# Block sums of w2 by accumulating transfers in GpSimd's queue, and the signs of seven products

## The chip, the cores and the metric

The kernel runs on one core of one Trainium2 chip. The metric is device time in microseconds (us) of one execution. The profiler records one further execution; its span is the time from the first to the last recorded instruction. PE is TensorE, DVE VectorE, ACT ScalarE, POOL GpSimd; SP issues the transfers of the kernel before.

## The reference

A layer norm feeds a linear attention block and a GELU feed-forward block; the second gates the first. S = 2048 rows, D = 576, 32 heads of 18, F = 4608, all in float32.

```python
x = A_x
xn = _layernorm(x, axis=-1)
s = _A_ref(xn, A_wqkv, A_wo)                     # phi(q) (phi(k)^T v) / (phi(q) sum phi(k)), then @ wo
h = gelu(xn @ w1 + b1)                           # 2048 x 4608
g = silu(h @ w2 + b2)                            # 2048 x 576
return x + s * g
```

## The kernel before

Float32 products are made on PE from split operands: `hi` is the value rounded by ACT to the type that PE multiplies, `lo` is the remainder, subtracted by DVE; a product is hi·hi + hi·lo + lo·hi. The large products are cut into 2 x 2 blocks and made with seven block products in place of eight (Strassen's scheme in Winograd's form), so sums of blocks of each operand are wanted as operands too. The second feed-forward product, `h @ w2`, takes four 128-row tiles of F at a time: a chunk `c` of nine. Its w2 operand has four blocks B(r, n) of 128 x 2 x 288 values in SBUF, r the row half and n the column half, and three sums of them.

The program has three stages.

1. **Keys and values** (to about 160 us): eight pairs of 128-row tiles. For a pair the rows are normalized (`x_stats`, with a power on POOL, L245; `x_norm` on ACT, L260), transposed on PE (`transpose_x`, L270), split and summed (`x_sum`, `s_hi`, `s_lo`), and projected. `s_lo` (L317 and L321) subtracts the remainders of x's sums on DVE.
2. **Queries and attention** (to about 290 us): rounds r = 0 to 9 of 14 places each. A round projects one pair's queries, divides (`den_sum` on DVE, `den_div` on POOL, L817), transposes the result of the pair before (L834, into one PSUM tile that `th` on ACT, L841, and `tl`, `th` on DVE, L845 and L846, must empty before the next), and multiplies it by the folded weights.
3. **Feed-forward**: 18 steps of 28 places, nine chunks for each half of the rows. A step makes two `Up` groups of seven products (`h`, L1118, with DVE's combinations L1138 to L1155 and the GELU on ACT, L1126), then, from place 14 on, the seven products with w2 (L1255), drained into `macc` by DVE (L1262).

Sums of w2's blocks are made at two places. `w2_load`, `w2_sum`, `w2_hi`, `w2_lo` (L473 to L503) run in stages 1 and 2: `SUMS` lists 19 (chunk, product) pairs, j = 0 to 18, and each is loaded, subtracted on POOL (L492), split on ACT (L496) and DVE (L501), and stored to DRAM. Class `W2` (from L1165) makes the others in the first half of stage 3, for the next chunk, as `sum7` (one subtraction, L1171) and `sum4` (two in a row, L1176 and L1177); `hi` and `lo` (L893, L896) split each operand, and the second half of the rows reads what was stored.

The order of work is written out by hand: `add(place, function, ...)` puts a function at a place, `at_step(place)` runs what stands there after a piece of PE's work, and every compute engine runs its own instructions strictly in that order, waiting at each until its inputs are there. In stages 1 and 2 this holds for the transfers of SP as well. The places of w2's sums:

```python
W2_FIRST = {2: (0,), 3: (1, 2), 4: (3,), 5: (4, 5), 6: (6,)}   # stage 1: pair -> sums j
    add(base + (1, 3)[n], w2_sum, j)
    add(base + (4, 9)[n], w2_hi, j)
    add(base + (6, 12)[n], w2_lo, j)
    add(base + ((0, 3) if r > 2 else (4, 5))[j], w2_sum, n + j)   # stage 2, rounds 2 to 7
    add(base + (7 if r > 2 else 10) + j, w2_hi, n + j)
    add(base + (9 if r > 2 else 11) + j, w2_lo, n + j)
```

Of the kernel before, what the change touches and what calls it, by code (L numbers as in the profile page):

```python
# [8 lines left out]
F32 = mybir.dt.float32  # L9
# [6 lines left out]
P = 128  # L16
S = 2048
D = 576
HD = 288
# [7 lines left out]
CF = 4  # L27
NC = NF // CF
# [14 lines left out]
def linear_attention_gated_ffn(ctx, tc, x, wqkv, wo, w1, b1, w2, b2, out):  # L43
    nc = tc.nc
    SUB, MUL, ADD = ALU.subtract, ALU.mult, ALU.add
# [254 lines left out]
    s_raw = scr[:, 1280 : 1280 + 9 * P].rearrange("p (k c) -> p k c", k=9)  # L300
# [14 lines left out]
    def s_lo(p):  # L315
        cs = pair_cols(p)
        nc.vector.tensor_tensor(  # L317
            xSL[:, :, cs], s_raw[:, :8], xSH[:, :8, cs].bitcast(F32), op=SUB
        )
        r = xSH[64:, 8, cs]  # L320
        nc.vector.tensor_tensor(r, s_raw[64:, 8], r.bitcast(F32), op=SUB)  # L321

    def x_store(p):
        cs = pair_cols(p)
# [139 lines left out]
    SUMS = [(0, 5), (0, 6), (0, 4)] + [(c, i) for c in range(1, NC) for i in (5, 6)]  # L464
    w2raw, w2op = {}, {}

    def w2_load(c, pool, tag):
        src = w2[c].rearrange("p (a r n d) -> p a r n d", a=2, r=2, n=2)
        if tag == "wa":
            tiles = [pool.tile([P, KT * 2 * P], F32, tag=tag, name=f"w2r{c}{r}") for r in range(2)]  # L470
            parts = [t[:, : 2 * D].rearrange("p (a n d) -> p a n d", a=2, n=2) for t in tiles]
            for r in range(2):
                nc.sync.dma_start(parts[r], src[:, :, r])  # L473
        else:
            t = pool.tile([P, CF * D], F32, tag=tag, name=f"w2r{c}")
            nc.sync.dma_start(t, w2[c])
            t = t.rearrange("p (a r n d) -> p a r n d", a=2, r=2, n=2)
            parts = [t[:, :, r] for r in range(2)]
        w2raw[c] = parts

    def w2_block(c, i):

        B = lambda r, n: w2raw[c][r][:, :, n, :]
        return {
            5: (B(0, 0), B(0, 1), B(0, 0)),
            6: (B(1, 1), B(1, 1), B(0, 0)), 4: (B(1, 0), B(1, 0), B(1, 1)),
        }[i]

    def w2_sum(j):
        c, i = SUMS[j]  # L490
        dst, a, b = w2_block(c, i)
        nc.gpsimd.tensor_tensor(dst, a, b, op=SUB)  # L492

    def w2_hi(j):
        w2op[j] = w1r.tile([P, 2, 2, HD], F32R, tag="stw", name=f"w2o{j}")
        nc.scalar.copy(w2op[j][:, 0], w2_block(*SUMS[j])[0])  # L496

    def w2_lo(j):
        c, i = SUMS[j]
        t = w2op.pop(j)  # L500
        nc.vector.tensor_tensor(t[:, 1], w2_block(c, i)[0], t[:, 0].bitcast(F32), op=SUB)  # L501
# [5 lines left out]
    def add(step, fn, *args):  # L507
        plans.setdefault(step, []).append((fn, args))
# [186 lines left out]
    for p in range(1, NPAIR):  # L695
        plan_pair(p)
        base = p * NSP
        if p > 1:
            pr = Proj(p, wkq, k_ts[p % 2], mu1)
            steps = [(pr.step, (i,)) for i in K_UP]  # L700
        else:
            pr = plain_k(p, 0)
# [6 lines left out]
        for s in range(2):  # L709
            pr = plain_v(p, s)  # L710
# [23 lines left out]
    base = NPAIR * NSP  # L734
    add(base + 1, finish_state)
    pr = Proj(Q_ORDER[0], wkq, q_tiles(0), mu2)
# [7 lines left out]
    w2rp = ctx.enter_context(tc.tile_pool(name="w2rp", bufs=1, reuse_waits="tile"))  # L744

    def load_w2_raw(n):
        raw = w2rp.tile([P, CF // 2, 2, 2, HD], F32, tag="w2raw", name=f"w2raw{n}")
        nc.sync.dma_start(raw.rearrange("p a b n d -> p (a b n d)"), w2[n % NC])
        return raw

    ph2 = ExitStack()
# [220 lines left out]
    for r in range(NPAIR + 2):  # L972
        base = (NPAIR + r) * NSP
# [3 lines left out]
        if r < NPAIR:  # L977
            a, b = q_tiles(r)
# [180 lines left out]
    class W2:  # L1159
# [4 lines left out]

        def load_raw(self):  # L1165
            self.raw = raw = load_w2_raw(self.n) if self.n else w2_raw0[0]
            self.B = lambda r, n: raw[:, :, r, n, :]
            self.src = {1: self.B(0, 0), 2: self.B(1, 0), 3: self.B(1, 1), 7: self.B(0, 1)}

        def sum7(self):  # L1170
            nc.gpsimd.tensor_tensor(self.src[7], self.src[3], self.src[7], op=SUB)  # L1171

        def sum4(self):
            tt = nc.gpsimd.tensor_tensor
            self.src[4] = self.src[2]
            tt(self.src[4], self.src[2], self.src[7], op=SUB)  # L1176
            tt(self.src[4], self.src[4], self.src[1], op=SUB)  # L1177

        def plain(self, f):
            self.src["p", f] = self.raw[:, f // 2, f % 2]  # L1180

        def hi(self, i):
            tag = ORDER[i[1]] if isinstance(i, tuple) else i
# [12 lines left out]
    class HOps:  # L1196
# [11 lines left out]
        def S(self, i, pr):  # L1208
            A = lambda r, c: self.A[pr, r, c]
            tt = nc.gpsimd.tensor_tensor  # L1210
            src = self.src
            if i == 5:
                src[5, pr] = A(1, 0)
                tt(src[5, pr], A(1, 0), A(1, 1), op=ADD)  # L1214
            elif i == 6:
                src[6, pr] = A(0, 0)
                tt(src[6, pr], src[5, pr], A(0, 0), op=SUB)  # L1217
            elif i == 3:
                src[3, pr] = A(0, 1)
                tt(src[3, pr], A(0, 1), src[6, pr], op=SUB)  # L1220
# [20 lines left out]
    CHAIN = {2: 1, 3: 5, 4: 7}  # L1241
    DST = {1: U1, 2: C11, 5: C22, 3: C12, 6: U1, 7: C22, 4: C21}
    BIAS = {2: 0, 7: 1, 3: 1, 4: 0}

    def product(c, i, q2, hs, w, held):

        wh, wl = w
        ps = held.pop((CHAIN[i], q2)) if i in CHAIN else bank2(f"pm{i}")
        if i in CHAIN.values():
            held[i, q2] = ps  # L1250
        for q in range(2):
            cs = slice((q2 + q) * P, (q2 + q + 1) * P)
            seq = [(st, m, p) for p in range(2) for st, m in ((0, wh), (0, wl), (1, wh))]
            for n, (st, m, p) in enumerate(seq):
                nc.tensor.matmul(  # L1255
                    ps[:, q, :HD], hs[p][st][:, cs], m[:, p, :],
                    start=(n == 0 and i not in CHAIN), stop=(n == len(seq) - 1),
                    skip_group_check=True,
                )
        src, dst = ps[:, :, :HD], macc[:, q2 : q2 + 2, DST[i], :]  # L1260
        if c > 0 or i in (5, 6):
            nc.vector.tensor_tensor(dst, src, dst, op=ADD)  # L1262
        elif i in BIAS:
            h = BIAS[i]
            bb = b2b[:, None, h * HD : (h + 1) * HD].to_broadcast([P, 2, HD])
            nc.vector.tensor_tensor(dst, src, bb, op=ADD)
        else:
            nc.vector.tensor_copy(dst, src)

    def combine(s, eng, q=slice(0, QH)):  # L1270
        A = lambda s: macc[:, q, s, :]
        eng.tensor_tensor(A(s), A(s), A(U1), op=ADD)

    def c_tile(bi, q):
        return macc[:, q, 2 * bi : 2 * bi + 2, :]
# [169 lines left out]
    for step in range(n_chunks):  # L1445
# [15 lines left out]
        if half == 0 and c < NC - 1:  # L1461
# [116 lines left out]
```

## Time and profile before

| what | value |
|---|---|
| median of 3 runs | 1120.35 us (1120.26 to 1120.59) |
| the profiled execution: its time | 1120.46 us |
| its span | 1118.8 us |
| POOL instructions that sum w2's blocks in stages 1 and 2 (L492) | 19, 29.8 us busy |
| POOL instructions that sum w2's blocks in stage 3 (L1171, L1176, L1177) | 25, 44.8 us busy |
| bytes moved by all transfers | 257.16 MB, mean 230 GB/s |
| transfers in POOL's queue | none |

A busy time counts what an engine executes, waits and issues of transfers left out. PE's instructions overlap, and their recorded lengths are longer than their pitch, so the pitch is read from the starts. An engine that is idle most of the time can still be one that another waits for; that is seen in the order of its instructions and in what ended the idle time before them.

### The profile page before, as it was taken

The page shows a single profiled execution, that of the slowest core. Times are in us where ns is not written, and L with a number is a line of the kernel's source. Part 1 is how long each engine was busy: PE and PEld are TensorE (multiplying, and loading weights), DVE is VectorE, ACT ScalarE, POOL GpSimd, SP SyncE. Part 2 cuts the span into 40 slices and gives each one's busy share as a digit, 9 for nine tenths or more (in the row PEclk, how much of TensorE's full clock was granted, in tenths as well). Part 3 has the DMA queues.
Part 4 walks back from the last instruction along what each step waited for, and adds up shares of the span by engine and source line. Part 5 has one row for each costly group of instructions (what it writes and reads, how often), then busy time and mean ns, then how long its engine had stood idle before and what let it go on. Part 6 is the DMA issues. An engine that isn't in the chain of part 4 may idle for free.

```text
span 1118.8 us, 18673 instructions
## 1 busy us (share of the span) xinstructions
PE 1099.8 (98%) x6924; PEld 1014.6 (91%) x6924; DVE 834.3 (75%) x1250; ACT 506.2 (45%) x913; POOL 485.2 (43%) x411
## 2 busy tenths in 40 slices
PE   8999999999999999999999999999999999999997
PEld 7899998999898998989989889899898998988987
DVE  6878756777598988989889888666475574664756
ACT  6766554445545454454454544524233242242352
POOL 5654434655364645645556443324224133242340
PEclk9999999999999999999999999999999999999999
DMA  5855537774968468385583759977666666666243
GB/s 202 289 210 224 223 99 238 279 281 161 354 253 322 179 234 296 153 326 193 207 323 149 294 181 369 373 261 267 217 207 215 211 200 210 228 200 222 88 136 119
DMA packets 89098, 257.16 MB, mean 230 GB/s; under 512 B 9581, under 2 KB 20333, under 8 KB 86959
## 3 DMA queue, kind: packets, MB, share of 16 engines
q1 hardware_dynamic: 89007, 255.96, 64.3%
q8 instruction: 55, 0.90, 0.3%
q14 instruction: 36, 0.29, 0.1%
HBM read 155.03 MB, written 100.01 MB: 228 GB/s over the span
## 4 chain that ended last, share of the span: by engine, by line
PE 82%; DVE 7%; ACT 4%; issue 2%; DMA 2%; POOL 2%; SPq 0%; DVEq 0%; POOLq 0%; ACTq 0%
PE pm L1255 32%; PE e L1118 12%; PE zy L1118 10%; PE a L1118 10%; PE b L1118 4%; PE pl L404 4%; PE ps_s L866 2%; PE pd L1372 2%; PE e L349 1%; DVE w2o L501 1%; DMA kr<-kw 1%; DVE h_l L896 1%; PE z L349 1%; PE ps_kva L457 1%; PE a L349 1%
## 5 line engine op out<-in xcount | busy, mean ns | idle before, releaser
L1262 DVE TENSOR_TENSOR macc<-pm,macc 128x576 f32<-128x576 f32 x218 | 164.1, 753 | 48.0 <-PE pm L1255 46.8
L893 ACT CAST h_h<-g 128x512 fp32r<-128x512 f32 x204 | 120.0, 621 | 142.2 <-PE pm L1255 141.1
L896 DVE TENSOR_TENSOR h_l<-g,h_h 128x512 fp32r<-128x512 f32 x204 | 171.2, 839 | 0.0
L1223 POOL TENSOR_TENSOR mid<-g 128x512 f32<-128x512 f32 x34 | 44.1, 1296 | 187.1 <-ACT g L1126 187.1
L1118 PE MATMUL a<-xH,wa 128*128 128x512 f32 x360 | 117.1, 390 | 0.0
L1118 PEld LDWEIGHTS a<-xH,wa 128*128 128x128 f32 x360 | 67.6, 188 | 13.6
L1126 ACT ACTIVATE g<-b,b1c 128x512 f32<-128x512 f32 x36 | 24.8, 689 | 121.5 <-DVE b L1144 121.5
L1118 PE MATMUL e<-xSH,wb 128*128 128x512 f32 x216 | 66.8, 390 | 0.9 <-DVE b L1144 0.9
L1343 POOL TENSOR_TENSOR fin1l<-fin1h,fin1l 128x288 f32<-128x288 f32 x8 | 6.5, 808 | 122.0 <-DMA fin1l<-s_dram 30.3
L1217 POOL TENSOR_TENSOR g<-g 128x512 f32<-128x512 f32 x34 | 49.6, 1459 | 20.8 <-DVE h_l L896 19.5
L1135 ACT COPY mid<-a 128x512 f32<-128x512 f32 x36 | 21.2, 588 | 78.5 <-PE a L1118 78.3
L1118 PE MATMUL a<-xL,wa 128*128 128x512 f32 x144 | 56.2, 390 | 0.0
L1220 POOL TENSOR_TENSOR g<-g 128x512 f32<-128x512 f32 x34 | 49.9, 1468 | 13.1 <-DVE h_l L896 11.8
L1214 POOL TENSOR_TENSOR g<-g 128x512 f32<-128x512 f32 x34 | 51.2, 1507 | 2.7
L1138 DVE TENSOR_TENSOR mid<-b,mid 128x512 f32<-128x512 f32 x36 | 24.7, 685 | 35.7 <-PE b L1118 33.3
L1118 PE MATMUL b<-xSH,w 128*128 128x512 f32 x144 | 50.2, 389 | 0.0
L1118 PE MATMUL zy<-xH,w 128*128 128x512 f32 x144 | 50.2, 389 | 0.0
L1118 PE MATMUL zy<-xSH,w 128*128 128x512 f32 x144 | 50.2, 389 | 0.0
L1118 PE MATMUL e<-xSH,w 128*128 128x512 f32 x144 | 50.2, 389 | 0.0
L1118 PEld LDWEIGHTS e<-xSH,wb 128*128 128x128 f32 x216 | 40.5, 188 | 10.1 <-DVE b L1144 1.7
L896 DVE TENSOR_TENSOR h_l<-mid,h_h 128x512 fp32r<-128x512 f32 x34 | 43.1, 1268 | 6.0 <-ACT h_h L893 6.0
L1126 ACT ACTIVATE g<-e,b1c 128x512 f32<-128x512 f32 x36 | 24.8, 689 | 48.8 <-DVE e L1151 48.8
(928 smaller groups left out, 3580.7 us busy)
## 6 DMA issues: line engine op xcount, KB each, us to landing
op<-w SPq DMA_DIRECT2D x72, 256.0 KB
w<-op SPq DMA_DIRECT2D x72, 256.0 KB
w1raw<-w SPq DMA_DIRECT2D x18, 640.0 KB
w2raw<-w SPq DMA_DIRECT2D x10, 1152.0 KB
op_a<-wa SPq DMA_DIRECT2D x18, 640.0 KB
wa<-op_a SPq DMA_DIRECT2D x18, 640.0 KB
op<-w2o SPq DMA_DIRECT2D x19, 576.0 KB
w2r<-w SPq DMA_DIRECT2D x6, 1152.0 KB
```

The source lines that it names most:

```text
L349: nc.tensor.matmul(ps, st, mv, start=first and n == 0, stop=n == len(seq) - 1, skip_group_check=True,)
L404: nc.tensor.matmul(self.ps[n], st, self.wk(hl, k, n), start=(i == 0), stop=(i == n_all - 1))
L893: nc.scalar.copy(pair[0], src)
L896: eng.tensor_tensor(pair[1], src, pair[0].bitcast(F32), op=SUB)
L1118: nc.tensor.matmul(ps.rearrange("p (c j) -> p c j", c=4), st, mv, start=first and n == 0, stop=n == len(seq) - 1, skip_group_check=True,)
L1126: nc.scalar.activation(g, ps, AF.Gelu_apprx_tanh, bias=b1c[:, f : f + 1])
L1214: tt(src[5, pr], A(1, 0), A(1, 1), op=ADD)
L1217: tt(src[6, pr], src[5, pr], A(0, 0), op=SUB)
L1220: tt(src[3, pr], A(0, 1), src[6, pr], op=SUB)
L1223: tt(src[7, pr], A(0, 0), A(1, 0), op=SUB)
L1255: nc.tensor.matmul(ps[:, q, :HD], hs[p][st][:, cs], m[:, p, :], start=(n == 0 and i not in CHAIN), stop=(n == len(seq) - 1), skip_group_ch ...
L1262: nc.vector.tensor_tensor(dst, src, dst, op=ADD)
```

## The change

All 44 subtractions of w2's blocks on POOL become transfers issued by POOL that add their source to what already lies in the target (`accum_op=ADD`). A transfer cannot subtract, so each product's w2 operand is now a sum, or stands with the opposite sign: the sums of `h` on POOL and the drains into `macc` change from addition to subtraction or back (`MINUS`, `combine`) on the same shapes. The host lays w2 out as r, n, a, d, so that a block is one run of 2304 bytes in each partition; a source is read from DRAM where a block as loaded is wanted, and from SBUF where it is itself a sum. `sum4` becomes two transfers into the same target, at places 22 and 24; the split of block 4 moves from places 24 and 25 to 27. The last part of `s_lo` (64 x 128) moves from DVE to POOL.

```diff
         r = xSH[64:, 8, cs]
-        nc.vector.tensor_tensor(r, s_raw[64:, 8], r.bitcast(F32), op=SUB)
+        nc.gpsimd.tensor_tensor(r, s_raw[64:, 8], r.bitcast(F32), op=SUB)
...
+    def w2_blocks(c):
+        return w2[c].rearrange("p (r n a d) -> p r n a d", r=2, n=2, a=2)
...
+    def add_to(dst, src):
+        nc.gpsimd.dma_start(dst, src, accum_op=ADD)
+
     def w2_sum(j):
         c, i = SUMS[j]
-        dst, a, b = w2_block(c, i)
-        nc.gpsimd.tensor_tensor(dst, a, b, op=SUB)
+        add_to(w2_block(c, i), {5: w2_blocks(c)[:, 0, 1], 6: w2_block(c, 5), 4: w2_block(c, 6)}[i])
...
         def sum7(self):
-            nc.gpsimd.tensor_tensor(self.src[7], self.src[3], self.src[7], op=SUB)
-
-        def sum4(self):
-            tt = nc.gpsimd.tensor_tensor
+            add_to(self.src[7], w2_blocks(self.n)[:, 1, 1])
+
+        def sum4(self, part):
             self.src[4] = self.src[2]
-            tt(self.src[4], self.src[2], self.src[7], op=SUB)
-            tt(self.src[4], self.src[4], self.src[1], op=SUB)
+            add_to(self.src[4], w2_blocks(self.n)[:, 0, 0] if part else self.src[7])
...
-                tt(src[5, pr], A(1, 0), A(1, 1), op=ADD)
+                tt(src[5, pr], A(1, 1), A(1, 0), op=SUB)
...
+    MINUS = (3, 5, 6, 7)
...
         if c > 0 or i in (5, 6):
-            nc.vector.tensor_tensor(dst, src, dst, op=ADD)
+            if i in MINUS:
+                nc.vector.tensor_tensor(dst, dst, src, op=SUB)
+            else:
+                nc.vector.tensor_tensor(dst, src, dst, op=ADD)
...
-            add(base + 22, nxt.sum4)
-            add(base + 24, nxt.hi, 4)
-            add(base + 25, nxt.lo, 4)
+            add(base + 22, nxt.sum4, 0)
+            add(base + 24, nxt.sum4, 1)
+            add(base + 27, nxt.hi, 4)
+            add(base + 27, nxt.lo, 4)
...
         "w2": np.ascontiguousarray(
-            np.asarray(B_w2, f32).reshape(NC, CF, P, D).transpose(0, 2, 1, 3)
+            np.asarray(B_w2, f32).reshape(NC, 2, 2, P, 2, HD).transpose(0, 3, 2, 4, 1, 5)
         ).reshape(NC, P, CF * D),
```

How the instructions move, in the program's order of an engine (not in time). First POOL at the end of a first-half step of stage 3, from block 7's sum on; w2raw is the next chunk's w2 as loaded, w1raw and w1t the next weights of w1 and their sums; in brackets the semaphores that an instruction waits for, DMAHW those of SP's transfers, DMASW those of POOL's. Before:

```order
L1171 TENSOR_TENSOR w2raw_6722<-w2raw_6722 128x2x288 [waits DMAHW2_49]
L1176 TENSOR_TENSOR w2raw_6722<-w2raw_6722 128x2x288 [waits DVE_49,Pool_49]
L1177 TENSOR_TENSOR w2raw_6722<-w2raw_6722 128x2x288 [waits Pool_49]
L918 TENSOR_TENSOR w1t_7000<-w1raw_6597 128x256 [waits DMAHW0_49]
L920 TENSOR_TENSOR w1t_7002<-w1raw_6597,w1t_7000 128x256 [waits Pool_49]
L923 TENSOR_TENSOR w1raw_6597<-w1raw_6597 128x256
```

And with the change:

```order
L490 DMA w2raw_6722<-w 128x576 [waits DMAHW2_49,DMASW5_49]
L490 DMA w2raw_6722<-w2raw_6722 128x576 [waits DMASW6_49,DVE_49]
L490 DMA w2raw_6722<-w 128x576 [waits DMASW7_49]
L920 TENSOR_TENSOR w1t_6998<-w1raw_6597 128x256 [waits DMAHW0_49]
L922 TENSOR_TENSOR w1t_7000<-w1raw_6597,w1t_6998 128x256 [waits Pool_49]
L925 TENSOR_TENSOR w1raw_6597<-w1raw_6597 128x256
```

The order is the same, but the second transfer now waits for the landing of the first and the third for that of the second, with the sums of w1 behind them.

Next ACT at the same place, where w_7 are operands of w2's next chunk, w_14 those of w1's next group, and mid<-a the first instruction for the next step's products. Before:

```order
L893 CAST h_h<-g 128x512 x3
L893 CAST w_7__6998<-w2raw_6722 128x576
L893 CAST w_14_7022<-w1t_7002 128x256
L893 CAST w_14_7041<-w1raw_6597 128x256
L893 CAST w_14_7043<-w1t_7000 128x256
L893 CAST wb_7067<-w1raw_6597 128x384
L893 CAST w_14_7069<-w1raw_6597 128x256
L1135 COPY mid<-a_7077 128x512
```

And with the change:

```order
L895 CAST h_h<-g 128x512 x3
L895 CAST w_14_7017<-w1t_7000 128x256
L895 CAST w_14_7036<-w1raw_6597 128x256
L895 CAST w_14_7038<-w1t_6998 128x256
L895 CAST w_7__7060<-w2raw_6722 128x576
L895 CAST wb_7067<-w1raw_6597 128x384
L895 CAST w_14_7069<-w1raw_6597 128x256
L1137 COPY mid<-a_7077 128x512
```

Block 4's split now stands behind three splits of w1; on DVE its remainder moves likewise, behind the last two drains into macc.

Last POOL in round 4 of stage 2, between the divisions of two rounds: w2r is a chunk of w2, pbuf the divided rows, e and scr the products for the next denominators. Before:

```order
L492 TENSOR_TENSOR w2r_2402<-w2r_2402 128x2x288 [waits DMAHW6_49]
L817 TENSOR_TENSOR pbuf_2024<-scr,den_2611 128x576 [waits DVE_49,PE_49,Pool_49]
L817 TENSOR_TENSOR pbuf_2025<-scr,den_2625 128x576 [waits DVE_49,PE_49,Pool_49]
L492 TENSOR_TENSOR w2r_2402<-w2r_2402 128x2x288 [waits Pool_49]
L804 TENSOR_TENSOR e_2026<-rt,zb 128x576 [waits Activation_49]
```

And with the change:

```order
L490 DMA w2r_2402<-w 128x576 [waits DMAHW6_49,DMASW0_49]
L819 TENSOR_TENSOR pbuf_2024<-scr,den_2611 128x576 [waits DVE_49,PE_49,Pool_49]
L819 TENSOR_TENSOR pbuf_2025<-scr,den_2625 128x576 [waits DVE_49,PE_49,Pool_49]
L490 DMA w2r_2402<-w2r_2402 128x576 [waits DMASW3_49]
L806 TENSOR_TENSOR e_2026<-rt,zb 128x576 [waits Activation_49]
```

Nothing changes place here; the second sum reads the first block where it lies and so waits for its transfer. The splits that follow on ACT (L496, now L498) and DVE keep their places.

More of the change, by code (lines that the diff above doesn't have):

```diff
@@ L746, in load_w2_raw @@
     def load_w2_raw(n):
-        raw = w2rp.tile([P, CF // 2, 2, 2, HD], F32, tag="w2raw", name=f"w2raw{n}")
-        nc.sync.dma_start(raw.rearrange("p a b n d -> p (a b n d)"), w2[n % NC])
+        raw = w2rp.tile([P, 2, 2, CF // 2, HD], F32, tag="w2raw", name=f"w2raw{n}")
+        nc.sync.dma_start(raw.rearrange("p r n a d -> p (r n a d)"), w2[n % NC])
         return raw
@@ L1271, in combine @@
         A = lambda s: macc[:, q, s, :]
-        eng.tensor_tensor(A(s), A(s), A(U1), op=ADD)
+        eng.tensor_tensor(A(s), A(s), A(U1), op=ADD if s == C21 else SUB)
     def c_tile(bi, q):
```

34 lines of the change are left out of this document (17 added, 17 removed).

## The prediction

> **What bounds the kernel now.** I read the page's head first, then the chain of waits in order of time, then the timelines of PE, DVE, ACT and POOL at the places that the change touches (columns there: start and length in us, engine, line, operation, what it writes and reads; in brackets the idle time before it and what ended it).
>
> ```profile
> span 1118.8 us, 18673 instructions
> PE 1099.8 (98%) x6924; PEld 1014.6 (91%) x6924; DVE 834.3 (75%) x1250; ACT 506.2 (45%) x913; POOL 485.2 (43%) x411
> ```
>
> TensorE is busy in 98% of the span and POOL in 43%, so work taken off POOL is worth nothing by itself. It is worth what it does to DVE or ACT where PE waits for them. The chain of waits in order of time (start, length, what) shows how much that can be:
>
> ```profile
> 589.05 13.07 PE pm L1255 x96
> 634.79 13.07 PE pm L1255 x96
> ...
> 860.93 22.39 PE pm L1255 x168
> 906.03 22.39 PE pm L1255 x168
> ```
>
> A step of the first half, where w2's sums are made, lasts 634.79 - 589.05 = 45.74 us; a step of the second half, with the same matmuls and ready operands, 906.03 - 860.93 = 45.10 us. So a first-half step loses 0.64 us, and eight of the nine first-half steps make the sums of a next chunk. The timelines of PE, DVE and POOL show one such loss:
>
> ```profile
> 605.55 0.43 PE L1255 MATMUL pm<-w__6695,h_h 128*128 128x288 f32 x2
> 606.07 0.40 PE L1255 MATMUL pm<-w__6695,h_l 128*128 128x288 f32 x1
> ...
> 603.49 0.68 DVE L896 TENSOR_TENSOR h_l<-g,h_h 128x512 fp32r<-128x512 f32 x1
> 604.76 1.26 DVE L896 TENSOR_TENSOR h_l<-g,h_h 128x512 fp32r<-128x512 f32 x1
> ...
> 603.72 1.75 POOL L1176 TENSOR_TENSOR w2raw<-w2raw 128x576 f32<-128x576 f32 x1 [4.74 <-DVE w__6936 L896]
> 607.26 1.19 POOL L918 TENSOR_TENSOR w1t<-w1raw 128x256 f32<-128x256 f32 x1
> ```
>
> The same DVE instruction takes 0.68 us with POOL still and 1.26 us beside POOL's sum; PE's h_l matmul starts at 606.07, just after it ends at 606.02. Its pitch before was 0.27 us for two, so PE lost about 0.25 us there; the rest of the 0.64 us lies at the like places a few microseconds earlier, where block 7's sum runs. Without POOL's reads DVE keeps up, and I count the whole 0.64 us as gain.
>
> **The unknown price: L, from the issue of an accumulating transfer to its landing.** The trace has no transfer in POOL's queue and none that adds. The nearest rows, from the chain and the page's list of issues:
>
> ```profile
> 0.80 2.85 DMA x<-x
> 199.89 7.58 DMA w2r<-w
> 232.10 4.55 DMA xSH<-x_dram
> ...
> x<-x SPq DMA_DIRECT2D x16, 288.0 KB
> xSH<-x_dram SPq DMA_DIRECT2D x4, 576.0 KB
> w2r<-w SPq DMA_DIRECT2D x6, 1152.0 KB
> ```
>
> A plain 288 KB load into a quiet machine took 2.85 us: the lower end. 1152 KB in the second stage took 7.58 us: the upper end. A sum brings 288 KB in and must also read the 288 KB that it adds to, so 576 KB at 4.55 us is nearest, and I take L = 4.5 us. POOL's own time for an issue lies between SP's (0.32 us, below) and the 1.43 us of the sum that it replaces; I take 1.0.
>
> The Trainium skill (DMA: Bandwidth & Descriptors, section "Anatomy of one DMA — SWDGE (gpsimd) path") fits a transfer from GpSimd's queue as about 2.0 us plus its bytes over 436 GB/s, which as an estimate is 2.7 us for 288 KB; no row here has such a transfer, and the fit is for plain ones. By it pair 2 below would cost 1.0 us, the rounds and steps would give 1.5 and 5.1 us back, and the sum would be -5.6 us.
>
> **The change part by part.**
>
> *First stage, pair 2.* The first sum stands in front of an ACT instruction that already waits for it, and a transposition on PE waits for what follows on ACT:
>
> ```profile
> 50.32 0.29 DVE L321 TENSOR_TENSOR xSH<-scr,xSH 64x128 fp32r<-64x128 f32 x1
> ...
> 60.00 1.43 POOL L492 TENSOR_TENSOR w2r<-w2r 128x576 f32<-128x576 f32 x1
> ...
> 61.46 0.68 ACT L496 CAST w2o<-w2r 128x576 fp32r<-128x576 f32 x1 [3.81 <-POOL w2r L492]
> 62.05 1.20 ACT L260 ACTIVATE xn<-x,mv 128x576 f32<-128x576 f32 x2
> 76.30 1.20 ACT L260 ACTIVATE xn<-x,mv 128x576 f32<-128x576 f32 x2
> ...
> 62.96 0.77 PE L270 MATMUL pt<-ident,xn 128*128 128x128 f32 x5
> 80.99 0.71 PE L270 MATMUL pt<-ident,xn 128*128 128x128 f32 x5
> ```
>
> The split waits for L in place of 1.43 us; behind it on ACT are the normalization, the exponentials and s_hi. PE gets xn L - 1.43 later, less 0.3 because L321 leaves DVE's part of this chain (50.32): at 4.5 us, **+2.8 us**. In pair 3 the same delay moves xn's end from 77.5 to about 80, and PE asks at 80.99: covered while L stays below about 5.7. There POOL's second sum waits for the first to land, and behind it stands the power for a later pair's variance, which waits for DVE's statistics anyway. The sums of pairs 4 and 5 stand as pair 3's do. L321's eight instructions go to a POOL that idles there: nothing on the path.
>
> *Second stage, rounds 3 to 7.* Each round sums one block early, with a whole half round until its split, and one late:
>
> ```profile
> 220.88 1.43 POOL L492 TENSOR_TENSOR w2r<-w2r 128x576 f32<-128x576 f32 x1
> ...
> 223.70 0.66 ACT L496 CAST w2o<-w2r 128x576 fp32r<-128x576 f32 x1
> 224.84 0.69 ACT L841 CAST th<-ptp 128x640 fp32r<-128x640 f32 x1
> ...
> 226.27 0.29 DVE L846 TENSOR_TENSOR th<-ptp,th 64x128 fp32r<-64x128 f32 x1
> 226.60 3.64 DVE L501 TENSOR_TENSOR w2o<-w2r,w2o 128x576 fp32r<-128x576 f32 x2
> ...
> 227.36 0.71 PE L834 MATMUL ptp<-ident,pbuf 128*128 128x128 f32 x5
> 233.34 0.29 PE L349 MATMUL z<-wkq_rl,xH 128*128 128x288 f32 x1
> 233.76 0.40 PE L349 MATMUL e<-wkq_h,xSH 128*128 128x288 f32 x1
> ```
>
> The late split can start at 220.88 + L, against 223.70: a shift of L - 2.82 = 1.7 us for s, th and DVE's L845 and L846. PE's next transposition reuses that PSUM tile, free at 226.57 and wanted at 227.36, so 0.8 us are covered and PE loses 0.9 us. DVE's two w2o subtractions, 1.8 us each beside POOL here, where a like one below (609.58) takes 1.00, win back about 1 us of the shift, so of PE's present wait between z and e (233.76 - 233.34, less a matmul's pitch of 13.07/96 = 0.14: 0.28 us) some 0.1 is left. Net 0.9 + 0.1 - 0.3 = 0.7 us, five rounds: **+3.5 us**. Cheaper transfers (shift under 0.8) would give -0.3 a round. Round 2's two sums stand further ahead of their splits, and I count nothing for them.
>
> *First half of the feed-forward part.* Block 7's sum goes out long before anything needs it, where before POOL waited 4.74 us behind it. The two parts of block 4's sum are serial, and POOL's weight sums, ACT's split of block 4 and DVE's remainder stand behind them:
>
> ```profile
> 609.58 1.00 DVE L896 TENSOR_TENSOR w__6998<-w2raw,w__6998 128x576 fp32r<-128x576 f32 x1
> 612.72 0.74 DVE L1262 TENSOR_TENSOR macc<-pm,macc 128x576 f32<-128x576 f32 x1
> 614.85 1.36 DVE L896 TENSOR_TENSOR wa<-w1raw,wa 128x640 fp32r<-128x640 f32 x1
> 616.13 0.68 DVE L1138 TENSOR_TENSOR mid<-b,mid 128x512 f32<-128x512 f32 x1
> 618.23 0.68 DVE L1144 TENSOR_TENSOR b<-e,mid 128x512 f32<-128x512 f32 x1
> ...
> 619.66 0.39 PE L1118 MATMUL e<-xSH,wb 128*128 128x512 f32 x1
> 603.60 0.32 SPq L890 DMA_DIRECT2D op<-w__6936  x1
> ```
>
> Part 0 goes out when DVE has finished with block 2, as the first sum at 603.72 did, a little earlier now: 603.4. Part 1 goes when it has landed, at 603.4 + L = 607.9; POOL's weight sums start an issue later, 608.9 against 607.26; part 1 lands at 603.4 + 2L = 612.4. DVE's weight remainders follow POOL by that 1.6 us, but block 4's remainder (1.00 us) no longer stands ahead of them and PE's products end 0.6 us sooner, so the last drain (612.72) ends at about 613.4 as before. Behind it now comes block 4's remainder, 0.7 us more ahead of wa's, L1138 and L1144. From the drain's end to L1144's end it was 618.91 - 613.46 = 5.5 us; with 0.7 more, and 0.2 less for the subtractions that POOL no longer slows, L1144 ends at 613.4 + 6.0 = 619.4, while PE, 0.64 earlier, wants E at 619.66 - 0.64 = 619.0: a wait of some 0.35 us. Net -0.64 + 0.35 = -0.3 a step, eight steps: **-2.3 us**. With L below about 4.2 the full -0.64 (-5.1 us); from L = 4.6 on the landing itself (then the split, 0.7 us) holds DVE up, and each 0.5 us of L costs a further 1 us a step. If that cover is gone the whole landing stands on PE's path.
>
> The rest costs nothing: the changed signs are the same instructions on the same shapes; w2's order in memory is made on the host; block 4's store moves past three stores and a load in SP's queue, and its reader is in the second half.
>
> Sum at L = 4.5: 2.8 + 3.5 - 2.3 = +4.0 us on the profiled execution's 1120.46 us (its span 1118.8): 1124.5; the median of the runs is 0.1 us lower, which changes nothing.
>
> **The rivals.**
> *Quick landing: faster.* At L = 3.5 pair 2 costs 1.8, the rounds give 5 x 0.3 = 1.5 back, the steps 5.1: -4.8, 1115.6 us. It decides below L = 3.9. For it: the 2.85 us row. Against it: the additional read of the target, and that the 4.55 us row comes from the stage in which the rounds' late sums go out. The fit that the Trainium skill gives (above) would land here. Chance 0.33.
> *The terms cancel.* L near 4.1: within 2 us, 1120.5. Chance 0.13.
> *Two slow landings stop the engines in order.* At L = 5.5 pair 2 costs 3.8, the rounds 5 x 1.7, and part 1 lands at 614.4, so that DVE starts block 4's remainder at 615.1 in place of 613.4: (0.35 + 1.7 - 0.64) x 8 = 11. Sum +23, 1143.5. For it: the 7.58 us row. Chance 0.12.
> *The sums weren't what slowed DVE*, so that h_l stays at 1.25 us and nothing is gained in the steps, where PE then also finds E ready: 2.8 + 3.5 = +6.3, 1127; the 0.68 beside the 1.26 speaks against it. It is inside the forecast's range.
>
> **How the numbers follow.** Forecast (L from 4.3 to 5.2) 0.42, its own range 1122.7 to 1136, centre 1124.5. All cases: from 1114.5 (L about 3.3) to 1143 (just under L = 5.5). About 0.2%, 2.2 us, can be told from no change: faster 0.33, same 0.13, slower 0.54.
>
> **What would show it.** Right: a gap of about 3 us on ACT ahead of the first L498 and on PE ahead of pair 2's transposition; ACT waiting for a DMA ahead of each round's second split; h_l near 0.7 us in the steps, with DVE waiting for block 4's split at their end. Wrong: landings under 3.9 us and first-half steps of 45.1 us, or steps longer than 46 us.

## The result, and the profile after

The changed kernel takes 1173.84 us (median of 6 runs, 1172.34 to 1177.54) against 1120.55 us (6 runs, 1120.26 to 1120.95): 1.0479 times as long, 95% interval 1.0464 to 1.0493. Its profiled execution has a span of 1172.0 us, 53.2 us more than before. First the head of its page, with the transfers by queue (packets, MB, share of the time of 16 DMA engines; q0 is POOL's queue, q1 SP's):

```profile
span 1172.0 us, 18759 instructions
PE 1113.1 (95%) x6924; PEld 1023.1 (87%) x6924; DVE 797.8 (68%) x1242; ACT 505.4 (43%) x913; POOL 453.0 (39%) x419
...
q1 hardware_dynamic: 88239, 255.96, 61.9%
q0 software_dynamic: 6336, 12.98, 7.3%
```

PE's work is the same 6924 matmuls, but it is busy 13.3 us longer while the span has grown by 53.2: most of the loss is PE standing still, and some of it is PE working slower. The table of waits on PE shows for whom it stood (line, then what it waited for, us in all, times, the longest):

```profile
PE e L1120 <- DVE b L1146: 15.0, 10, 1.9
PE ptp L836 <- DVE th L848: 10.9, 3, 4.6
PE pt L270 <- ACT xn L260: 5.0, 3, 3.3
PE z L349 <- ACT s L876: 4.7, 1, 4.7
PE b L1120 <- ACT w L895: 4.2, 7, 0.8
```

Before, the longest wait in this table was 1.7 us. The three stages are all here: pt is the first, ptp and z the second, e and b the feed-forward part. Comparing the start of the same matmul in both traces gives the loss by place: +5.9 us at the end of the first stage, +25.3 at the first feed-forward product, +30.0 at the first step's products with w2 (314.72 before, 344.74 after), +53.2 from the eighth step's on (634.79, 688.03), and nothing in the second half of the rows. So the stages cost 6, 19 and 28 us, the last as 4.7 in the first step and 23.2 in the next seven.

The price that the prediction did not have stands in the table of issues (queue, count, size, median us from issue to landing) and, one by one, in the chain of waits:

```profile
w2raw<-w POOLq DMA_DIRECT2D x17, 288.0 KB, 4.5
w2r<-w2r POOLq DMA_DIRECT2D x10, 288.0 KB, 5.1
w2r<-w POOLq DMA_DIRECT2D x9, 288.0 KB, 6.1
w2raw<-w2raw POOLq DMA_DIRECT2D x8, 288.0 KB, 6.3
```

```profile
93.78 7.97 DMA w2r<-w
201.47 5.44 DMA w2r<-w2r
232.64 7.98 DMA w2r<-w2r
271.66 8.07 DMA w2r<-w2r
320.63 10.04 DMA w2raw<-w
639.73 12.88 PE pm L1256 x96
654.47 6.32 DMA w2raw<-w2raw
688.03 12.88 PE pm L1256 x96
702.77 3.67 DMA w2raw<-w2raw
```

The same 288 KB took from 3.67 to 10.04 us in these rows, and from 3.44 to 10.04 over all 44 transfers. One step in the timeline of POOL, ACT and PE (the step whose products with w2 start at 639.73) shows what stands behind a landing:

```profile
654.47 0.86 POOL L490 DMA_DIRECT2D w2raw<-w2raw  x1 [5.82 <-DVE w__6936 L898]
661.18 0.86 POOL L490 DMA_DIRECT2D w2raw<-w  x1 [5.85 <-DMA w2raw<-w2raw]
661.74 1.07 POOL L920 TENSOR_TENSOR w1t<-w1raw 128x256 f32<-128x256 f32 x1
...
663.65 0.41 ACT L895 CAST w<-w1t 128x256 fp32r<-128x256 f32 x1 [7.33 <-POOL w1t L922]
665.70 0.68 ACT L895 CAST w__7060<-w2raw 128x576 fp32r<-128x576 f32 x1 [0.65 <-DMA w2raw<-w]
...
664.11 0.50 PE L1120 MATMUL b<-xSH,w 128*128 128x512 f32 x1 [0.52 <-ACT w L895]
672.75 0.50 PE L1120 MATMUL e<-xSH,wb 128*128 128x512 f32 x1 [1.92 <-DVE b L1146]
```

Part 0 of sum 4 goes out at 654.47 and part 1, which must wait for it, at 661.18. POOL does nothing in between, and the sums of w1 behind it start 661.74 - 639.73 = 22.0 us after the step's first product, where before it was 607.26 - 589.05 = 18.2. ACT waits 7.33 us for the first of them, and PE twice: for the split (b) and for what DVE makes of it (e). For block 4 itself ACT waits only 0.65 us.

The other part of the loss is the clock. This table of stretches gives for each its busy time by engine and, third from the right, the TensorE clock granted in it:

```profile
core 0: us, PE busy (x) PEld busy (x) DVE busy (x) ACT busy (x) POOL busy (x), PEclk, DMA share, GB/s
203.70:207.11 3.41, 0.00 (x0) 0.00 (x0) 2.08 (x1) 0.17 (x1) 2.30 (x3) 1.00 0.61 114
207.11:213.94 6.83, 5.98 (x25) 5.98 (x26) 5.55 (x12) 2.29 (x6) 1.27 (x2) 0.50 1.03 322
374.36:377.78 3.42, 1.51 (x8) 0.92 (x6) 3.28 (x6) 0.10 (x2) 0.74 (x1) 1.00 0.98 379
377.78:381.19 3.41, 3.41 (x8) 2.69 (x9) 2.12 (x5) 3.32 (x7) 0.00 (x0) 0.50 1.02 380
671.32:674.74 3.42, 1.99 (x9) 1.64 (x10) 2.22 (x5) 2.01 (x4) 0.00 (x0) 1.00 1.09 412
674.74:678.15 3.41, 3.41 (x17) 2.82 (x16) 3.18 (x6) 1.98 (x5) 0.00 (x0) 1.00 0.94 344
```

In the stretch after one in which PE stood still or worked 1.51 us of 3.42, the clock is half. Seven times before the program's end this happens, 30.7 us in all. PE is busy in 26.8 us of them, which at half speed is worth up to 13.4 us of the 53; its busy time grew by about as much (13.3). The wait in front of e is the same 2 us in every step; it halves the clock when it falls into one stretch (374.36) and not when it straddles two (671.32: PE still worked 1.99 us). So seven like steps cost 2.4 to 2.8 us, or 4.1 to 4.5 with a halved stretch.

### The profile page after: what moved, and what is told of

It reads as the page before. It is cut to its first block, busy times and chain, and to the rows that moved or that the text cites. A ratio compares the mean times of both kernels' runs of the same rounds, so it can differ in the third digit from the quotient of the medians.

```text
span 1172.0 us, 18759 instructions
## 1 busy us (share of the span) xinstructions
PE 1113.1 (95%) x6924; PEld 1023.1 (87%) x6924; DVE 797.8 (68%) x1242; ACT 505.4 (43%) x913; POOL 453.0 (39%) x419
## 3 DMA queue, kind: packets, MB, share of 16 engines
q1 hardware_dynamic: 88239, 255.96, 61.9%
q0 software_dynamic: 6336, 12.98, 7.3%
## 4 chain that ended last, share of the span: by engine, by line
PE 69%; DMA 13%; DVE 8%; ACT 4%; issue 3%; POOL 2%; DVEq 0%; POOLq 0%; ACTq 0%
PE pm L1256 26%; PE e L1120 10%; PE zy L1120 8%; PE a L1120 7%; DMA w2raw<-w2raw 4%; DMA w2raw<-w 3%; PE pl L404 3%; PE b L1120 3%; PE ps_s L868 3%; DMA w2r<-w2r 2%; DMA w2r<-w 2%; PE e L349 2%; PE pd L1379 2%; PE a L349 1%; PE z L349 1%
## 5 line engine op out<-in xcount | busy, mean ns | idle before, releaser
L898 DVE TENSOR_TENSOR h_l<-g,h_h 128x512 fp32r<-128x512 f32 x204 | 158.7, 778 | 0.0
L1264 DVE TENSOR_TENSOR macc<-macc,pm 128x576 f32<-128x576 f32 x128 | 95.8, 749 | 36.7 <-PE pm L1256 36.6
L1120 PE MATMUL e<-xSH,wb 128*128 128x512 f32 x216 | 70.4, 409 | 15.0 <-DVE b L1146 15.0
L1266 DVE TENSOR_TENSOR macc<-pm,macc 128x576 f32<-128x576 f32 x90 | 67.9, 754 | 18.4 <-PE pm L1256 17.1
L1140 DVE TENSOR_TENSOR mid<-b,mid 128x512 f32<-128x512 f32 x36 | 24.6, 684 | 35.4 <-PE b L1120 35.4
L1153 DVE TENSOR_TENSOR e<-e,mid 128x512 f32<-128x512 f32 x36 | 25.1, 698 | 31.5 <-PE e L1120 31.2
```

Source lines behind the costliest of these rows:

```text
L898: eng.tensor_tensor(pair[1], src, pair[0].bitcast(F32), op=SUB)
L1120: nc.tensor.matmul(ps.rearrange("p (c j) -> p c j", c=4), st, mv, start=first and n == 0, stop=n == len(seq) - 1, skip_group_check=True,)
L1264: nc.vector.tensor_tensor(dst, dst, src, op=SUB)
```

## The experiments

Where a text names theories: A, the waits in the engines' order, with the halved clock behind them; B, the signs, places and L321 by themselves; C, the transfers' traffic, wherever they run.

**Which part costs what.** In four kernels the sums are made by POOL's instructions again, in all places or in some; the signs, the layout and the places stay changed.

```diff
-            add_to(self.src[7], w2_blocks(self.n)[:, 1, 1])
+            nc.gpsimd.tensor_tensor(self.src[7], self.src[7], self.src[3], op=ADD)
...
-            add_to(self.src[4], w2_blocks(self.n)[:, 0, 0] if part else self.src[7])
+            nc.gpsimd.tensor_tensor(self.src[4], self.src[4], self.src[1 if part else 7], op=ADD)
```

> All of w2's sums by GpSimd's instructions again, with the changed signs, the changed places (sum 4 in two parts, its split and remainder in slot 27) and L321 on GpSimd. Theory A (the time went to waits for the landings and to the lowered clock behind PE's pauses): 1118 to 1122 us, clock 1.0 throughout. Theory B (the changed signs, the later slot or L321 cost by themselves): 1130 us or more. Theory C (the transfers load the DMA engines and memory while others run): 1118 to 1122 too.

> Transfers in the feed-forward part alone; the sums of the first two stages by GpSimd's instructions. Theory A: the last matmuls of the changed kernel came 27.9 us later than where its second stage ended (53.2 - 25.3), so 1120.4 + 28 = 1148 us, steps of 48.2 us, or 50.2 where the clock is halved, as in the changed kernel. Theory B: like the run with all sums on GpSimd. Theory C: in proportion to the transfers, 17 + 8 of 44, so 53 x 25/44 = 30: 1150; it does not tell A from C.

> Transfers in the first two stages alone. Theory A: 1120.4 + 25.3 = 1146 us, +6 of it in the first stage and +19 in the second, each behind a wait of ACT for a landing. Theory C: 53 x 19/44 = 23: 1143. If the two halves do not add up to the 53 us, the waits of one stage hide behind those of the other.

> Only block 7's sum by a transfer (nine transfers), every other sum by GpSimd's instructions. Nothing waits for block 7 for some 10 us after its issue. Theory A: no loss, and DVE's h_l beside that sum back to 0.68 us: 1116 to 1121 us. Theory C: nine transfers of 44 cost 53 x 9/44 = 11: 1131 us.

With all sums on POOL: 1120.14 us, ratio 0.9998 (0.9985 to 1.0011). B falls: signs, layout, places and L321 together cost 1.2 us at most, the upper end of the interval. Transfers in the feed-forward part alone: 1144.8 us, 1.0213 (1.0186 to 1.024); in the first two stages alone: 1144.37 us, 1.02 (1.0173 to 1.0226), +25.1 in its trace at the end of the second stage, as in the changed kernel (25.3). The two losses add to 48 us, with fewer halved stretches in the first of them. These two runs do not tell A from C, which had forecast 1150 and 1143. Block 7's sum alone: 1122.91 us, 1.0014 (1.0004 to 1.0023), which both theories missed; C falls, since it had 11 us for these nine transfers and 2.3 were lost. Its trace has 3.4 us more of waits in the first step (waits of PE are counted here from one start to the next, less the usual pitch; that is some 0.15 us more than the idle time that a row shows), where chunk 0's block 7 goes out at place 2 and its split stands at place 4, and steps of 45.53 us after that, 0.2 less than before: A holds but for a place that I had overlooked.

**The first step.** Chunk 0's block 7 goes back to POOL (`if self.n:` ahead of the transfer).

> As the run with transfers in the feed-forward part alone, with chunk 0's block 7 (issued in the first step) summed by GpSimd's instruction. PE's three waits in the first step are 1.4, 1.8 and 1.6 us there, and 0.9 in all before the change. Theory A: they go, 1144.8 - 3.9 = 1141 us. Theory C: no change beyond one transfer of 25, -1 us.

1145.58 us, 1.0218 (1.0189 to 1.0248): no gain in the total, though the trace shows the waits gone (0.9 us left, and the step's first product at 316.17 where block 7 by transfer had 318.96). Three of its later steps met the halved clock, against one, and at the change to the second half of the rows PE waited 1.9 us for a load, which it did not there. A kernel whose PE waits near the edge of halving is timed by where the stretches fall.

**What holds a step.** Three kernels move pieces of sum 4: its parts swapped; part 1 behind the first sums of w1; that, with block 4's split in the next step. The second fence below is the edit of the last of them; the kernel before it has its first two lines alone.

```diff
-            add_to(self.src[4], w2_blocks(self.n)[:, 0, 0] if part else self.src[7])
+            add_to(self.src[4], self.src[7] if part else w2_blocks(self.n)[:, 0, 0])
```

```diff
-            add(base + 24, nxt.sum4, 1)
+            add(base + 26, nxt.sum4, 1)
...
-            add(base + 27, nxt.hi, 4)
-            add(base + 27, nxt.lo, 4)
+            add(base + NS + 5, nxt.hi, 4)
+            add(base + NS + 5, nxt.lo, 4)
```

> As the run with transfers in the feed-forward part alone, with the two parts of sum 4 in the other order: first block (0,0) from DRAM (4.4 us), then block 7 from SBUF (6.5 us). GpSimd stands 2.1 us less before its weight sums; the second landing, and so block 4's split, comes when it did. Theory A1 (the weight sums queued behind the wait on GpSimd cost the steps): PE's two waits in a step, 0.7 and 2.05 us, shrink by up to 2.1, steps of 45.5 to 46.2 us, total 1127 to 1131. Theory A2 (block 4's own landing, then its split and remainder ahead of wa's, costs them): only the 0.7 goes, steps of 47.5, total about 1139 us. Theory C (traffic): no change, 1144.

> As the run with transfers in the feed-forward part alone, with part 1 of sum 4 two slots later, behind GpSimd's first weight sums, so that these wait for nothing. Part 1 still cannot start before part 0 has landed, so block 4's split comes no earlier. Theory A1: steps of 45.5 to 46.2 us, total 1127 to 1131. Theory A2: the E wait of 2.05 us stays, steps of 47.5 or more, total 1139 us or more.

> As the run with part 1 behind the first weight sums, and block 4's split and remainder not at the step's end but five slots into the next step, so that ACT and DVE do not wait for the landing in front of wb and wa. Chunk 0's block 7 stays a transfer. Theory A1 and A2 together: no wait is left in the steps but h_l beside the weight sums (0.42 us); steps of 45.7 to 46.0; 1120.4 + 4 for the first step + 0 to 2 = 1124.5 to 1126.5 us. If it is the traffic: as that run, 1138.

Swapped: 1156.64 us, 1.0319 (1.0298 to 1.0341), worse, against every theory. Part 0 from DRAM now took some 7 us (in eight steps POOL waited 50.8 us for it behind the issues, in the changed kernel 44.6 for part 0 from SBUF) and part 1 from SBUF was there when ACT asked. It is the place that is slow and not the source. Part 1 behind the weight sums: 1138.55 us, 1.0166 (1.0143 to 1.0189), on A2's side. The b wait went, but ACT now waits for block 4's landing with wb and wa behind it:

```profile
440.22 0.67 ACT L896 CAST w__5060<-w2raw 128x576 fp32r<-128x576 f32 x1 [6.88 <-DMA w2raw<-w]
```

With the split moved too: 1130.2 us, 1.0077 (1.0062 to 1.0092), steps of 46.5 us. Both waits are gone; 0.42 us stay in front of h_l, beside which the sums of w1 now run, and 0.66 in front of e in the next step, where block 4's remainder now stands on DVE. So two things were queued behind the landings, the weight sums first and block 4 close behind.

**Starting earlier.** Two kernels spread the transfers over the step, both with chunk 0's block 7 on POOL.

> As the run before this one, and in every other step block 7's transfer eight slots earlier, block 2's split and remainder six, part 0 of sum 4 six and part 1 two, so that both landings (6.5 + 0.35 + 4.4 us) lie behind the 22 us of the seven products before GpSimd's weight sums. Theory A: no wait is left, and DVE runs beside no sum of GpSimd's: 1120.4 - 8 x 0.4 = 1117 us, down to 1115.5 if the whole 0.64 us a step comes back; 1123 if block 2's remainder, earlier on DVE, costs PE 0.75 us a step. Theory C: transfers cost wherever they run: 1140 us.

> Transfers in the feed-forward part alone, chunk 0's block 7 by GpSimd, and in each step: block 7's transfer four slots earlier, behind GpSimd's last sums for h (the run that put it eight earlier stopped GpSimd at the load of the chunk, with h's sums behind it); block 2's split and remainder four slots earlier; part 0 from DRAM right behind them, part 1 from SBUF two slots before GpSimd's weight sums; block 4's split and remainder five slots into the next step. Theory A1 and A2 (waits in the engines' order): neither wait is left; steps of 45.3 to 45.7 us, total 1117 to 1121. If a landing of 6.5 us or more still reaches the weight sums: steps of 46.5, total 1127. Theory C (traffic of the transfers itself): 1140.

Block 7 eight places earlier: 1160.58 us, 1.0341 (1.0305 to 1.0378). The timeline of POOL says why:

```profile
369.94 0.91 POOL L490 DMA_DIRECT2D w2raw<-w  x1 [5.47 <-DMA w2raw<-w]
370.56 1.61 POOL L1227 TENSOR_TENSOR mid<-g 128x512 f32<-128x512 f32 x1
```

The chunk's own load had not landed; POOL waited 5.47 us for it with a sum for h (L1227) behind, and PE with it. Block 7 four places earlier, behind those sums: 1128.85 us, 1.0065 (1.005 to 1.008), steps of 46.65 us, no halved clock. What is left is two waits of 0.7 us for DVE, for a drain and for b, ahead of which the remainders of blocks 2 and 4 now stand: not landings any more.

**The second stage.** Only the sum issued early in a round is a transfer (with `c > 2`, which takes in round 2's first sum as well: six transfers).

> In rounds 3 to 7 of the second stage only the sum issued early in a round (block 5, a half round ahead of its split) is a transfer; all others are GpSimd's instructions. Theory A (the second stage's +19 us comes from the late sum, whose split waits): 1119 to 1121 us, no halved clock. Theory C: five transfers of 44, +6, 1126.

1122.2 us, 1.0005 (0.9995 to 1.0015). Round 3's landing took 9.59 us and cost PE 2.7; the four rounds after it gained some 0.4 us each. So the late sums, round 2's among them, had made the 19 us. An early one is free only while it lands in time: 9.59 us was too long in round 3, and 7.87 us in a later kernel was not.

**The landing by itself.** Transfers into a tile that nothing else uses.

> All sums by GpSimd's instructions, and in five steps of the second half, where no sums are made, transfers of 288 KB into a tile that nothing else uses: from GpSimd's queue adding from DRAM, adding from SBUF, copying from DRAM, copying from SBUF; from SyncE's queue copying from DRAM and from SBUF; and one adding from DRAM right behind loads of 864 KB. Theory Q (the queue has the price): the four of GpSimd's queue alike, 4.4 to 6.5 us, SyncE's near 2.9. Theory R (the read of the target has it): the adding ones slower than the copying ones of the same queue by a microsecond or more. Theory S (the source in SBUF has it): both from SBUF near 6.5, both from DRAM near 4.4. Theory T (what else is in flight): all near 3.5 to 4.5, the one beside the loads 7 to 10. The total is not compared; it may be a few us longer.

The view of a source line (instruction lengths in ns, then us to the landing): L1461 adds from DRAM, L1464 adds from SBUF, L1467 copies from DRAM, L1470 copies from SBUF, all in POOL's queue.

```profile
L1461 POOL DMA_DIRECT2D probe<-w x2: 876/880/883, 784.0 to 873.6; - x2
DMA to landing us min/median/max: 6.4/7.4/8.4
```

```profile
L1464 POOL DMA_DIRECT2D probe<-probe x2: 890/892/895, 807.6 to 897.8; - x2
DMA to landing us min/median/max: 3.8/3.8/3.8
```

```profile
L1467 POOL DMA_DIRECT2D probe<-w x2: 609/612/616, 820.2 to 910.4; - x2
DMA to landing us min/median/max: 3.8/3.9/3.9
```

```profile
L1470 POOL DMA_DIRECT2D probe<-probe x2: 577/577/577, 824.5 to 914.7; - x2
DMA to landing us min/median/max: 2.9/3.2/3.4
```

S falls: adding from SBUF takes 3.8 us here and 6.3 in the steps. Q alone falls too, since one queue gives 2.9 to 8.4. R (adding is slower than copying) is left open: adding took 0.6 us more than copying from SBUF and 3.5 more from DRAM, two transfers of each in differing company. The transfers meant to be beside the big loads (4.4 to 5.1 us) were not: SP's order isn't written by hand here, and it had issued those loads 7 us or more ahead. So the probe did not settle T. SP's landings are not in the trace.

**What is in flight beside it.** In the last step with sums part 0 took 3.67 us, and there the 576 KB store of block 2's operand is missing. Two runs tried to take that store away from part 0, and one moved part 0, all with chunk 0's block 7 on POOL (1145.58 us without them).

```diff
+            add(base + 25, nxt.store, 2)
```

> As the run with transfers in the feed-forward part and chunk 0's block 7 by GpSimd (1145.6 us), with the store of block 2's operand to DRAM (576 KB, SyncE's queue) four slots later, so that it is not in flight beside part 0 of sum 4. Theory T (the landing takes as long as what is in flight beside it makes it): part 0 lands in 3.7 to 4.0 us in place of 6.3 to 6.6, part 1 goes out 2.6 us earlier, GpSimd's weight sums begin 19.3 us after a step's first product instead of 21.9 (18.2 before the change), steps of 45.6 to 46.5 us, no halved clock: 1120.4 + 0 to 6 = 1120 to 1127 us. Theory S or Q (the source or the queue has the price): no change, 1140 to 1146.

1142.51 us, 1.0188 (1.0171 to 1.0205), but the edit did nothing: SP's order isn't written by hand in this part, and SP's instructions kept it. The store still went out at once, the 576 KB load behind it, and part 0 between them (timelines of SP and POOL):

```profile
425.02 0.32 SPq L893 DMA_DIRECT2D op<-w__4936  x1
425.41 0.88 POOL L490 DMA_DIRECT2D w2raw<-w2raw  x1 [5.84 <-DVE w__4936 L899]
426.76 0.32 SPq L1202 DMA_DIRECT2D w__4976<-op  x1
```

It is the run with chunk 0 on POOL once more (1145.58 us), and the 3 us between the two show how much the halved clock scatters such a kernel. So the store went to ACT's queue, which runs in the order written:

```diff
+                nc.scalar.dma_start(d, self.tiles[2].bitcast(F32))
...
+            add(base + 27, nxt.store_2)
```

> As the run with transfers in the feed-forward part and chunk 0's block 7 by GpSimd (1145.6 us), with block 2's store issued from ACT's queue, behind the splits of the weight sums, so that it cannot be in flight beside part 0 of sum 4; the load of 576 KB still is. Theory T (bytes in flight set the landing): part 0 lands in 3.7 to 4.4 us (3.67 in the last step of the changed kernel, where that store is missing), GpSimd's weight sums begin 19.4 us after a step's first product in place of 21.9, steps of 45.4 to 46.5: 1118 to 1127 us. Theory S or Q (source or queue): 6.3 us, 1140 to 1146.

1121.0 us, 0.9997 (0.9988 to 1.0006): 24.6 us won by moving one transfer. Its timeline of POOL:

```profile
420.43 0.88 POOL L490 DMA_DIRECT2D w2raw<-w2raw  x1 [5.86 <-DVE w__4936 L899]
424.58 0.88 POOL L490 DMA_DIRECT2D w2raw<-w  x1 [3.27 <-DMA w2raw<-w2raw]
425.15 1.07 POOL L921 TENSOR_TENSOR w1t<-w1raw 128x256 f32<-128x256 f32 x1
```

Part 0 lands in 3.7 to 3.8 us in seven of eight steps, and in 4.4 in the other. SP's load of 576 KB still goes out 1.35 us behind part 0 (421.78, and 426.76 against 425.41 in the run before), so only the store is gone. This step's products start at 405.67, so the weight sums begin 19.5 us later; the steps take 45.6 to 46.4 us, most of them 45.7. T holds for this place: without the store beside it the 6.3 us are gone.

**Part 0 earlier** (block 2's split by one place, part 0 by two, from 22 to 20), in the kernel with the store edit that changed nothing; block 7 and the second stage's early sums alone (`c > 3`: rounds 3 to 7, five transfers, not four); and both.

```diff
-            add(base + 21, nxt.hi, 2)
-            add(base + 21, nxt.lo, 2)
-            add(base + 22, nxt.sum4, 0)
+            add(base + 20, nxt.hi, 2)
+            add(base + 20, nxt.lo, 2)
+            add(base + 20, nxt.sum4, 0)
```

> As the run with block 2's store later, with block 2's split, its remainder and part 0 one slot earlier, so that GpSimd's weight sums begin about 18.2 us after a step's first product, as before the change. If the wait on GpSimd is what is left there: steps of 45.4 to 45.7 us, 1117.5 to 1120.5. If it is block 4's remainder at the step's end: as the run before, 1 us or less better. Block 2's remainder may delay h_l on DVE by up to 0.7 us a step, as it did four slots earlier: 1125.

> Transfers only where nothing waits for them for 10 us: block 7's sums from chunk 1 on, and the early sum of rounds 4 to 7 in the second stage; all others by GpSimd's instructions. From the runs before: 0.13 us a step for block 7 (eight) and 0.3 us a round (four), so 1120.4 - 2.2 = 1118.2 us; no halved clock but where the first stages already reach one. If the traffic costs anything by itself, 1120.5 or more.

> As the run with block 2 one slot earlier (1115.6 us), and the early sum of rounds 4 to 7 of the second stage by a transfer too. The run with block 7 and these early sums gained 0.3 us a round of the second stage: 1115.6 - 1.2 = 1114.4 us if the gains add up.

Part 0 earlier: 1115.58 us, 0.9945 (0.9928 to 0.9962), faster than both kernels. The timelines of SP and POOL:

```profile
417.10 0.32 SPq L893 DMA_DIRECT2D op<-w__4919  x1
420.44 0.32 SPq L1202 DMA_DIRECT2D w__4976<-op  x1
...
417.49 0.88 POOL L490 DMA_DIRECT2D w2raw<-w2raw  x1 [4.25 <-DVE w__4919 L899]
422.22 0.87 POOL L490 DMA_DIRECT2D w2raw<-w  x1 [3.85 <-DMA w2raw<-w2raw]
422.80 1.07 POOL L921 TENSOR_TENSOR w1t<-w1raw 128x256 f32<-128x256 f32 x1
```

Here the store is still beside part 0, but the load follows 3 us later, and the landing takes 4.3 us (3.8 to 4.3 over the steps with a store). So the 6.3 us took the store and the load close together. The rate alone does not set it: the DMA engines moved 224 to 243 GB/s during these landings, and 226 to 239 during the slow ones of the changed kernel. The weight sums start 422.80 - 404.35 = 18.5 us after the step's first product, and a step takes 45.18 us, with no wait of PE over 0.2 us in it: the whole 0.64 us but for 0.08 has come. Transfers only where nothing waits for them: 1117.37 us, 0.9962 (0.9948 to 0.9975), 0.8 below its forecast. Both together: 1114.5 us, 0.9943 (0.9928 to 0.9958), the fastest that was found; the last microsecond of it is inside the intervals.

## Why the prediction was wrong

**Direction right, size far off.** It said 1124.5 us, slower by 4, with a chance of 0.54 for slower at all; it was 53 slower and outside the range. The feed-forward part was to give 2.3 us back and cost 28, so the right direction was in part luck.

**The step that failed** is "A sum brings 288 KB in and must also read the 288 KB that it adds to, so 576 KB at 4.55 us is nearest, and I take L = 4.5 us". One number stood for 44 transfers. Where little else was in flight 4.5 was right (block 7's and part 1's median); beside a store and a load of 576 KB each it was 6.3, in the second stage 4.7 to 8.1 but for the last, at the first step 10.0. The range failed with it: it ended just under L = 5.5, though the prediction had named 7.58 us as the upper end of L. That row, "1152 KB in the second stage", was read as a price of bytes, but 288 KB took as long there. That company made it so is shown for part 0 alone, where what was in flight was varied. For the rest it is argued from the rates: the 22 landings of up to 4.64 us lie in stretches of 64 to 169 GB/s, the 16 of more than 6 in stretches of 226 to 343 (and a rate alone, as shown above, does not set a landing).

**By term.** *The rounds* had the right mechanism. Late split against transposition, less 2.82 and 0.8 us of cover, gives for the landings of 7.98 and 8.07 us waits of 4.4 and 4.5; PE waited 4.6 and 4.4. For 5.85 us it gives 2.2, and PE waited 2.0; the other two (4.74 and 3.48 us) cost no wait, where it gives 1.1 for the first. At L = 4.5 it gave 0.9. *Round 2*, counted at nothing, cost 4.7 us: its second sum waits on POOL for the first one's landing, ACT's split then waits for its own, and behind that split stands the s that PE wants.

```profile
201.47 0.89 POOL L490 DMA_DIRECT2D w2r<-w2r  x1 [4.94 <-DMA w2r<-w]
206.94 0.67 ACT L498 CAST w2o<-w2r 128x576 fp32r<-128x576 f32 x1 [4.48 <-DMA w2r<-w2r]
```

*Pair 2*: 2.8 forecast, 3.3 measured, and a halved stretch behind it. The pairs after it were to be covered "while L stays below about 5.7" (its own rows give 5.2: 80.99 - 77.50 + 1.43 + 0.3); pair 4's took 7.97 and cost 1.2.

**The steps.** The -0.64 us was right, as the kernel with part 0 earlier shows. Wrong was the 0.35 against it. I had the weight sums 1.6 us late and the bound at block 4's own landing; they were 3.8 us late and themselves the bound (ACT waited 7.33 us for them, 0.65 for block 4). So it was not the size of L alone: with the measured 6.3 and 4.4 us the prediction's own rule gives, as an estimate, 1.1 us a step, and without a halved stretch 2.4 to 2.8 were lost. The runs give the slope: weight sums at 18.2 to 18.5, 19.4 and 22.0 us make steps of 45.2, 45.7 and 48.3. The first two are other kernels, with other differences too, but the changed kernel's own last step, at 19.4, takes 45.7 as well. Up to 19.4 half a microsecond is lost, beyond that each microsecond costs one.

**Two terms were missing.** Chunk 0's block 7, which "goes out long before anything needs it" in the other steps, is issued two places ahead of its split in the first (4.7 us); and the halved clock (up to 13.4 us), which in the trace of before, always at 1.00 until the last microseconds, was not to be seen. The Trainium skill has it (TensorE: Matmul & The Clock Gate, section "What's actually happening"): a free-running window of 3413 ns and half the clock after an idle one. The length agrees with the 3.41 us here; that the stretch has to be idle does not, since PE was busy for 1.51 us of the one at 374.36.

**The rival "Two slow landings stop the engines in order"** was the right story, at 0.12 and too small: it set L = 5.5 everywhere and asked nothing of the clock. The fit of the Trainium skill (DMA: Bandwidth & Descriptors, section "Anatomy of one DMA — SWDGE (gpsimd) path"), 2.7 us for 288 KB as an estimate, would have erred further: the probe's plain copies took 2.9 to 3.9 us, and no adding transfer less than 3.4.

## What to carry to other kernels

A transfer that replaces an instruction is priced by its landing beside whatever else is in flight at that moment, and by everything queued behind the first engine that must wait for it: here one 576 KB store beside it was worth 24.6 us. Give it room for the longest landing that the traces show (10 us here, where 4.5 is common), order serial ones so that no engine has other work behind the wait, and look first at the one with the least room (here the first step's). Where PE is nearly always busy, price a pause of two microseconds at up to twice its length, since the clock may be halved behind it.

## What had not been expected of the hardware

- **Half an idle stretch is enough.** Over the 19 traces of before, after and all experiments, cut along the 3.41 us grid on which the clock changes, the last 20 us of each left out: of the stretches at full clock in which PE's matmuls were busy for less than 45%, 26 of 26 were followed by a halved one; of those between 45 and 55%, 14 of 27; of those above, none of 6063.
- **POOL's issue is longer for adding.** 880 to 890 ns against 577 to 612 for a plain copy, in the probe.
- **A byte costs more in POOL's queue.** After: 12.98 MB took 7.3% of the DMA engines' time, 0.56% a MB, and SP's 255.96 MB 61.9%, 0.24% a MB. Whether that is the addition or the smaller packets was not tried.
- **From SBUF adding is quicker, where little else moves.** In the kernel with block 7 eight places earlier, part 0 from SBUF took 3.43 to 3.51 us and part 1 from DRAM 4.29 to 4.50.
- The probe's two adds from DRAM took 6.4 and 8.4 us and its adds from SBUF 3.8; what was beside them was not taken apart.
